# Sigmoid attention and a bilinear feed-forward on one core: sums of the late weights' blocks in buffers of their own, their w_out part stored in 2 KB rows, eight warm-up matmuls, first v on ScalarE's queue

## The chip, the core and the metric

One NeuronCore of a Trainium2 chip runs the kernel as one program. TensorE (PE in the rows, PEld for its weight loads) multiplies into PSUM; VectorE (DVE), ScalarE (ACT) and GpSimd (POOL) do the elementwise work; SyncE (SP) only issues transfers. ScalarE and GpSimd issue transfers too, each in the order of its own queue, and all transfers are moved by the core's 16 DMA engines. Every engine takes its instructions strictly in program order, so an instruction that waits holds up all that stand behind it on its engine. The metric is the device time of one execution in microseconds (us), lower is better.

## The reference

Shapes: q, k, v are 8 x 12 x 448 x 64 (batch, heads, sequence, head size), x has 3584 tokens of 768, w1 and w2 are 768 x 1024, w3 is 1024 x 1024 and w_out 1024 x 768. The weights are given in float64 (their reference arithmetic runs on them), everything else in float32.

```python
scores = scale * np.matmul(q, k.transpose(0, 1, 3, 2)) - np.log(S)
attn = 1.0 / (1.0 + np.exp(-scores))
x = np.matmul(attn, v).astype(np.float32)   # heads side by side: 3584 x 768
a = x @ w1
b = x @ w2
h = a * b @ w3
return (h @ w_out).astype(np.float32)
```

## The kernel before, in words

The program has four stages, which TensorE goes through one after the other.

**Attention** (0 to 257 us in the profile). 48 pairs of heads; for each, scores (L174, L190 for the short last chunk), a sigmoid on ScalarE (L182), and the product with v (L201, L208). The result x goes to DRAM (x_dram). Ahead of the first scores TensorE runs 13 matmuls on a tile of zeros (L318), so that its clock is up when real work begins. The loads of the first four pairs are all issued by SyncE, q and k of a pair and then its v, save k of pair 0, which ScalarE issues. Beside the attention, w1 and w2 are decoded from their float64 words (`piece_load`, `piece_magnitude`, `piece_decode`), split into a high and a low part (each product is made as three float32r matmuls) and summed for the next stage.

**Units** (258.7 to 703.1 us). a = x w1 and b = x w2, and their product g, with Winograd's form of Strassen's scheme: seven block products instead of eight. There are 16 groups (4 token blocks x 4 pairs of column blocks of the result). A group is seven steps, `names` = a11, a12, s3, s2, s1, a22, s4; a step is `unit_step` for two column blocks, each 9 matmuls (L428) into one PSUM bank. VectorE takes the results out of PSUM (`add`, L435): u and v of s2, r of a12 and s1, v of a22, u of s4. ScalarE copies a11's result (L443, tile u). GpSimd multiplies the finished halves (L458 after a22, L463 after s4) and issues the store of g (L465). The step s4 accumulates into the very banks of s1 (`kept`), so its first matmul has to wait until VectorE has read s1's result out of that bank (r of s1).

Beside the units, the late weights w_out and w3 are prepared by a generator, `decode_late`, from which the loop over the groups takes a step at a time (`take(decodes, 1)` at three places of most groups). Each block of 128 x 512 numbers is loaded by SyncE (raw, two buffers), ScalarE makes the magnitude (L84, into a tile f, five buffers), VectorE decodes it in six instructions (L91 to L107). From four decoded blocks b11, b12, b21, b22 of a column block, four sums are made **in place**: t3 = b22 - b12 is written over b12, t2 = b11 + t3 over b11, t1 = b22 - t2 over b22, n4 = b21 - t2 over b21 (L477 for differences, L435 for the sum). The blocks b11, b22 and b21 themselves are needed too, so they are put on a list (`put`, `settled`) and stored to DRAM by GpSimd (`store_settled`, L492) one step of the loop later; a sum over such a block has to wait until the store has read it. The first 12 blocks are w_out's (into wo_dram, whose layout makes each store 512 rows of 512 bytes), the next 16 w3's (into w3_dram, 128 rows of 2 KB each).

**Composition** (703.1 to 761.5 us). The product w3 w_out in seven products (L762), each with operands that `load_factors` loads from wo_dram (L568, L569) and w3_dram (L573), three products ahead, and splits on ScalarE, VectorE and GpSimd.

**Output** (761.5 us to the end). g times the composed weight, again seven products (L821).

What sets the order: in attention the program text sets it for every engine. In the units it sets it for TensorE and SyncE alone, and a list scheduler of the framework orders VectorE, ScalarE and GpSimd from its own estimates of the times; so the place at which a decode or a sum stands in VectorE's queue is the scheduler's choice, and the change moves it. A tile of a pool with n buffers waits for the last readers of the tile n allocations before it.

The lines that the change touches: L70 (layout of wo_dram), L144 to L157 (the table load of the sigmoid, and `load_v`), L268 to L270 (when piece 0 is decoded), L311 to L318 (first loads, warm-up), L442 (buffers of u), L501 to L552 (the sums), L568 and L569 (the factors' loads).

Of the kernel before, what the change touches and what calls it, by code (L numbers as in the profile page):

```python
# [11 lines left out]
F32 = mybir.dt.float32  # L12
F32R = mybir.dt.float32r
U32 = mybir.dt.uint32
AF = mybir.ActivationFunctionType
# [10 lines left out]
def sigmoid_attention_bilinear_ffn(  # L26
# [16 lines left out]
    nc = tc.nc  # L43
    B, H, D, S = qT.shape
    DM, DF = w1.shape[0], w1.shape[1] // 2
    NT = B * S
    P = 128
    CHUNKS = [(c, min(P, S - c)) for c in range(0, S, P)]
    NC = len(CHUNKS)
# [3 lines left out]
    NF = DF // P  # L53
    NM = DM // 2
    NH = NF // 2
# [7 lines left out]
    const = ctx.enter_context(tc.tile_pool(name="const", bufs=1))  # L63
    pw = ctx.enter_context(tc.tile_pool(name="pw", bufs=6))
    dram = ctx.enter_context(tc.tile_pool(name="dram", bufs=1, space=bass.MemoryType.DRAM))
# [1 line left out]
    g_dram = dram.tile([NF, P, NT], F32, name="g_dram")  # L67
    t_dram = dram.tile([NF, 4, P, 2, KH, P], F32, name="t_dram")
    w3_dram = dram.tile([7, NF // 2, P, NF // 2, P], F32, name="w3_dram")
    wo_dram = dram.tile([7, P, NF // 2, NM], F32, name="wo_dram")  # L70
    corner_dram = dram.tile([P, NF // 2, NM], F32, name="corner_dram")

    def split(dst_hi, dst_lo, src, hi_engine, lo_engine):
# [8 lines left out]
    def magnitude(raw, pool, bufs):  # L82
        f = pool.tile([P, *raw.shape[1:-1]], F32, name="f", bufs=bufs)
        nc.scalar.activation(f, raw[..., 1].bitcast(F32), AF.Abs, scale=HW_SCALE)  # L84
        return f
# [38 lines left out]
    pa = phase_a.enter_context(tc.tile_pool(name="pa", bufs=2, side="left"))  # L124
    ps = phase_a.enter_context(tc.tile_pool(name="ps", bufs=3, space=PSUM))

    PLAIN = 1
    pairs = [(b, hp) for b in range(B) for hp in range(NPAIR)]

    def load_pair(p, engines=(nc.sync, nc.sync)):  # L130
        b, hp = pairs[p]
        heads = slice(2 * hp, 2 * hp + 2)
        qk = pa.tile([P, 2, S], F32, name="qk", bufs=6)
        for i, (src, engine) in enumerate(zip((qT, kT), engines)):
            engine.dma_start(out=qk[:, i], in_=src[b, heads].rearrange("h d s -> (h d) s"))
        return qk
# [4 lines left out]
    bias = const.tile([P, 1], F32, name="bias")  # L141
    nc.vector.memset(bias, -math.log(S))

    ready = const.tile([P, 1], F32, name="ready")  # L144
    nc.scalar.activation(ready, bias, AF.Sigmoid)

    def load_v(p):
        b, hp = pairs[p]
        vv = pa.tile([P, NC, 2 * D], F32, name="vv", bufs=6)
        cols = slice(hp * 2 * D, (hp + 1) * 2 * D)  # L150
        full = (NC - 1) * P
        nc.sync.dma_start(
            out=vv[:, :NC - 1], in_=v[b, :full, cols].rearrange("(c p) e -> p c e", p=P)
        )
        rows = slice(p % 2 * D, (p % 2 + 1) * D)
        nc.sync.dma_start(out=vv[rows, NC - 1], in_=v[b, full:, cols])
        return vv  # L157

    def split_pair(p, qk):
# [106 lines left out]

    steps = []
    for i in range(2 * NF):  # L268
        at = 2 + 5 * i // 2
        steps += [(max(at - 3, 0), piece_load, (i,)), (at - 1, piece_magnitude, (i,)), (at, piece_decode, (i,))]  # L270
        steps += [(at + 1, piece_split, (i,))]
        if i % 2:
            steps += [(at + 1, piece_sum, (i // 2, 0)), (at + 2, piece_sum, (i // 2, 3))]
            steps += [(at + 2, piece_sum, (i // 2, 2)), (at + 3, piece_sum, (i // 2, 1))]
# [33 lines left out]
    order.enter_context(tc.manual_schedule(engines={ET.PE, ET.SP, ET.Activation, ET.Pool}))  # L308
    AHEAD = 4
    X_LOADS = 2 * NPAIR + 8  # L310
    qks[1] = load_pair(1)  # L311
    vvs[0] = load_v(0)
    vvs[1] = load_v(1)
    for p in range(2, AHEAD):
        qks[p], vvs[p] = load_pair(p), load_v(p)
    warm = ps.tile([P, 2, 512], F32, name="sp", bufs=3)
    for _ in range(13):
        nc.tensor.matmul(warm[:, 0, :S], zeros[:, :P], zeros, start=True, stop=True)  # L318
    parts = {0: (qks[0],)}
    xs = []  # L320
# [113 lines left out]
    def add(out, a, b):  # L434
        nc.vector.tensor_tensor(out=out, in0=a, in1=b, op=ALU.add)  # L435
# [3 lines left out]
    def unit_step(g, fc, name):  # L439
        acc = x_product(fc, name)  # L440
        if name == "a11":
            us[fc] = pu.tile([P, S], F32, name="u", bufs=3)  # L442
            nc.scalar.copy(out=us[fc], in_=acc)  # L443
        elif name == "a12":
            rs[fc] = pu.tile([P, 2, S], F32, name="r", bufs=3)
            add(rs[fc][:, 0], acc, us[fc])
        elif name == "s3":
            p7s[fc] = acc
        elif name == "s2":
            add(us[fc], acc, us[fc])  # L450
            vs[fc] = pu.tile([P, S], F32, name="v")
            add(vs[fc], p7s.pop(fc), us[fc])
        elif name == "s1":
            add(rs[fc][:, 1], acc, vs[fc])
        elif name == "a22":
            add(vs[fc], acc, vs[fc])
            r = rs[fc]
            nc.gpsimd.tensor_tensor(out=r[:, 1], in0=r[:, 1], in1=vs.pop(fc), op=ALU.mult)  # L458
        else:
            u = us.pop(fc)  # L460
            add(u, acc, u)
            r = rs.pop(fc)
            nc.gpsimd.tensor_tensor(out=r[:, 0], in0=r[:, 0], in1=u, op=ALU.mult)  # L463
            at = 2 * g * S
            nc.gpsimd.dma_start(  # L465
                out=g_dram[fc, :, at:at + 2 * S].rearrange("p (t s) -> p t s", t=2), in_=r
            )
# [8 lines left out]
    def subtract(out, a, b):  # L476
        nc.vector.tensor_tensor(out=out, in0=a, in1=b, op=ALU.subtract)  # L477
# [16 lines left out]
    def decode_late():  # L494
        todo = list(late_sources())
        nxt = [load_words(todo.pop(0), pu, 2) for _ in range(2)]
        yield

        def one():
            raw = nxt.pop(0)  # L500
            f = decode(raw, magnitude(raw, pu, 5))  # L501
            if todo:
                nxt.append(load_words(todo.pop(0), pu, 2))
            return f

        for cb in range(NM // P):
            def put(name, f):
                settled.append((wo_dram[right[name], :, :, cb * P:(cb + 1) * P], f))

            b12 = one()  # L510
            yield
            b11 = one()
            put("b11", b11)
            yield
            b22 = one()
            put("b22", b22)
            subtract(b12, b22, b12)
            put("t3", b12)
            yield
            add(b11, b12, b11)  # L520
            put("t2", b11)
            subtract(b22, b22, b11)
            put("t1", b22)
            b21 = one()
            put("b21", b21)
            yield
            subtract(b21, b21, b11)
            put("n4", b21)
            yield
        for c in range(NH):  # L530
            def put(name, f):
                settled.append((w3_dram[left[name], c], f))

            a21 = one()
            yield
            a11 = one()
            put("a11", a11)
            subtract(a21, a11, a21)
            put("s3", a21)
            yield  # L540
            a22 = one()
            put("a22", a22)
            yield
            subtract(a22, a22, a21)
            put("s2", a22)
            add(a11, a22, a11)
            put("s1", a11)
            a12 = one()
            put("a12", a12)
            yield  # L550
            subtract(a12, a12, a22)
            put("s4", a12)  # L552
            yield

    arenas = (("x1", "x2", "a11"), ("a12", "s3", "s2"), ("s1", "a22", "s4"))
# [3 lines left out]
    def load_factors(i):  # L559
        t0, t1, t2 = (  # L560
            arena_pools.get(tag, px2).tile([P, 6 * S], F32R, name="ar", tag=tag, bufs=1)
            for tag in arenas[i % len(arenas)]
        )
        J = NH - 1
        wide, one = J * NM, NH * P
        out_hi, out_lo = ([t[:, k * w:(k + 1) * w] for t, w in ((t0, wide), (t1, NM))] for k in range(2))
        at = 2 * NM
        nc.sync.dma_start(out=out_lo[0].bitcast(F32), in_=wo_dram[i, :, :J].rearrange("p j m -> p (j m)"))  # L568
        nc.sync.dma_start(out=out_lo[1].bitcast(F32), in_=wo_dram[i, :, J])  # L569
        hi3 = [t1[:, at:at + one], t2[:, :one], t2[:, 2 * one:3 * one], t2[:, 4 * one:5 * one]]  # L570
        lo3 = [t1[:, at + one:at + 2 * one], t2[:, one:2 * one], t2[:, 3 * one:4 * one], t1[:, at + 2 * one:at + 3 * one]]
        for c, lo in enumerate(lo3):
            nc.sync.dma_start(out=lo.bitcast(F32), in_=w3_dram[i, c].rearrange("p j m -> p (j m)"))  # L573
        for hi, lo in zip(out_hi, out_lo):
            split(hi, lo, lo.bitcast(F32), nc.scalar.copy, nc.vector)
        for c, (hi, lo) in enumerate(zip(hi3, lo3)):
            split(hi, lo, lo.bitcast(F32), nc.scalar.copy, nc.gpsimd if c > 1 else nc.vector)

        def moving(k, j):
            t = (out_hi, out_lo)[k]  # L580
            return t[0][:, j * NM:(j + 1) * NM] if j < J else t[1]

        def standing(k, c, j):
            return (hi3, lo3)[k][c][:, j * P:(j + 1) * P]

        loaded[i] = (moving, standing)
# [330 lines left out]
```

## Time and profile before

| what | before |
|---|---|
| median of 3 runs | 968.41 us (966.88 to 973.74) |
| the profiled execution | 971.64 us, its span 969.8 us |
| TensorE busy | 928.5 us (96%) |
| VectorE, ScalarE, GpSimd busy | 714.6, 384.3, 156.8 us |
| mean granted clock of TensorE | 0.981 |
| stages: attention, units, composition, output | 0 to 257, 258.7 to 703.1, to 761.5, to 969.8 us |

The span runs from the first to the last instruction; the execution's own time is 1.84 us longer. Busy TensorE time is counted with each matmul's end as modelled, so a slow matmul counts as busy: time lost to a low clock is not in the 4% that TensorE sits idle. The row of the granted clock stands in tenths in the profile, and by stretch in the view by windows.

### The profile page before, as it was taken

How to read it: one execution, taken by the hardware profiler on the slowest of the kernel's cores; microseconds unless marked ns; L12 is line 12 of the kernel's file. 1: busy time of each engine (PE TensorE's matmuls, PEld its weight loads, DVE VectorE, ACT ScalarE, POOL GpSimd, SP SyncE). 2: the span in 40 equal slices, each digit the busy share in tenths (PEclk: the TensorE clock that was granted, in tenths of full speed). 3: DMA queues.
4: the chain of work that ended last, by engine and by line, in shares of the span. 5: the costliest groups of instructions: out<-in, count | busy, mean ns of one | idle time of the engine just before them, and what ended most of it. 6: DMA issues, size and time to landing. Idle time of an engine off the chain costs nothing.

```text
span 969.8 us, 14374 instructions
## 1 busy us (share of the span) xinstructions
PE 928.5 (96%) x5191; PEld 760.4 (78%) x5191; DVE 714.6 (74%) x1084; ACT 384.3 (40%) x544; POOL 156.8 (16%) x165
## 2 busy tenths in 40 slices
PE   9999999999996798967999999999999999999998
PEld 5455455455695798967999999899999998999997
DVE  5889898986583759727697679756569998777762
ACT  6878878877810013100230113000466544233310
POOL 0000000000031332413323232234344000000000
PEclk9999999999998899987999999999999999999999
DMA  9888999995288465882758866677787367565622
GB/s 298 263 294 288 307 326 322 326 320 199 102 281 326 137 229 178 280 303 99 241 177 300 322 233 204 233 244 238 240 271 255 104 208 245 183 235 183 216 89 86
DMA packets 134134, 227.59 MB, mean 235 GB/s; under 512 B 11632, under 2 KB 100080, under 8 KB 134064
## 3 DMA queue, kind: packets, MB, share of 16 engines
q1 hardware_dynamic: 127152, 197.34, 61.0%
q0 software_dynamic: 6768, 29.10, 8.2%
q8 instruction: 42, 0.69, 0.3%
q14 instruction: 28, 0.23, 0.1%
q10 hardware_dynamic: 144, 0.23, 0.1%
HBM read 163.71 MB, written 62.91 MB: 234 GB/s over the span
## 4 chain that ended last, share of the span: by engine, by line
PE 70%; DVE 13%; issue 8%; DMA 5%; POOL 2%; ACT 2%; DVEq 0%; POOLq 0%; ACTq 0%
PE up L428 26%; PE up L821 16%; PE av L208 11%; PE sp L174 10%; PE av L201 2%; PE sp L190 2%; DMA wo_dram<-f 1%; DVE w L75 1%; DMA ar<-wo_dram 1%; DMA w_dram<-f 1%; DVE u L435 1%; PE up L762 1%; DVE r L435 1%; ACT ar L74 1%; DVE gs L75 1%
## 5 line engine op out<-in xcount | busy, mean ns | idle before, releaser
L428 PE MATMUL up<-xs,tw 128*128 128x448 f32 x864 | 175.7, 362 | 0.2 <-DVE u L435 0.2
L428 PEld LDWEIGHTS up<-xs,tw 128*128 128x128 f32 x864 | 161.9, 187 | 11.4 <-DVE u L435 0.6
L182 ACT ACTIVATE ap<-sp,bias 128x896 f32<-128x896 f32 x168 | 156.2, 1008 | 14.5 <-PE sp L174 10.8
L428 PE MATMUL up<-xa,w 128*128 128x448 f32 x576 | 117.9, 362 | 0.7 <-ACT t L214 0.7
L821 PE MATMUL up<-gs,w 128*128 128x448 f32 x576 | 116.6, 362 | 2.0 <-DVE v L653 2.0
L821 PEld LDWEIGHTS up<-gs,w 128*128 128x128 f32 x576 | 107.9, 187 | 9.6 <-ACT gs L74 2.3
L428 PEld LDWEIGHTS up<-xa,w 128*128 128x128 f32 x576 | 107.9, 187 | 8.6 <-ACT t L214 1.5
L208 PE MATMUL av<-ap,vv 128*64 128x448 f32 x576 | 113.5, 543 | 0.0
L84 ACT ACTIVATE f<-raw 128x512 f32<-128x512 f32 (+1 forms) x44 | 33.8, 769 | 193.2 <-DMA raw<-w3T 124.1
L428 PE MATMUL up<-xs,w 128*128 128x448 f32 x288 | 66.9, 389 | 33.3 <-DVE r L435 33.3
L458 POOL TENSOR_TENSOR r<-r,v 128x448 f32<-128x448 f32 x32 | 42.8, 1357 | 341.3 <-DVE v L435 341.2
L428 PEld LDWEIGHTS up<-xs,w 128*128 128x128 f32 x288 | 58.5, 205 | 39.7 <-DVE r L435 35.1
L208 PEld LDWEIGHTS av<-ap,vv 128*64 128x64 f32 x576 | 39.2, 137 | 63.5 <-issue 54.4
L821 PE MATMUL up<-ga,w 128*128 128x448 f32 x432 | 88.2, 363 | 0.0
L821 PEld LDWEIGHTS up<-ga,w 128*128 128x128 f32 x432 | 81.0, 188 | 6.0
L477 DVE TENSOR_TENSOR f<-f 128x512 f32<-128x512 f32 x21 | 14.6, 697 | 79.9 <-DMA wo_dram<-f 48.2
L428 PE MATMUL up<-xa,tw 128*128 128x448 f32 x288 | 60.2, 362 | 0.0
L762 PE MATMUL up<-ar 128*128 128x384 f32 x336 | 58.4, 334 | 0.0
L762 PEld LDWEIGHTS up<-ar 128*128 128x128 f32 x336 | 58.3, 188 | 0.0
L174 PE MATMUL sp<-qh 64*128 64x448 f32 x282 | 57.7, 406 | 0.0
L428 PEld LDWEIGHTS up<-xa,tw 128*128 128x128 f32 x288 | 54.0, 187 | 3.6
L174 PEld LDWEIGHTS sp<-qh 64*128 64x128 f32 x282 | 26.3, 183 | 37.9 <-issue 31.7
(88 smaller groups left out, 1299.6 us busy)
## 6 DMA issues: line engine op xcount, KB each, us to landing
tw<-t_dram SPq DMA_DIRECT2D x128, 384.0 KB, 5.0
graw<-g_dram SPq DMA_DIRECT2D x60, 448.0 KB, 4.4
g_dram<-r POOLq DMA_DIRECT2D x32, 448.0 KB, 3.1
raw<-w SPq DMA_DIRECT2D x16, 768.0 KB, 6.6
t_dram<-th SPq DMA_DIRECT2D x32, 384.0 KB, 4.4
qk<-qT SPq DMA_DIRECT2D x48, 224.0 KB, 4.7
x_dram<-t SPq DMA_DIRECT2D x48, 224.0 KB, 5.0
xr<-x_dram SPq DMA_DIRECT2D x48, 224.0 KB, 6.1
```

The costliest lines, as they stand in the source:

```text
L75: lo_engine.tensor_tensor(out=dst_lo, in0=src, in1=dst_hi, op=ALU.subtract)
L84: nc.scalar.activation(f, raw[..., 1].bitcast(F32), AF.Abs, scale=HW_SCALE)
L174: nc.tensor.matmul(sp[:, j], qks[kt][rows, 1, at:at + n], qks[qt][rows, 0], start=m == 0, stop=m == len(terms) - 1,)
L182: nc.scalar.activation(a, sp, AF.Sigmoid, bias=bias, scale=scale)
L190: nc.tensor.matmul(sp[i * D:(i + 1) * D, j], qk[rows, 1, S - D:], qk[rows, 0], start=True, stop=True)
L201: nc.tensor.matmul(acc[cols, :S], v[rows, NC - 1, cols], a[rows, j], start=True, stop=False)
L208: nc.tensor.matmul(acc[cols, :S], v[:, c, cols], a[:, j], start=False, stop=c == len(aps) - 1)
L428: nc.tensor.matmul(acc[:, :S], ws[w][:, c], xop[name][x][:, c], start=onto is None and (c, m) == (0, 0), stop=(c, m) == (KH - 1, 2), skip_ ...
L435: nc.vector.tensor_tensor(out=out, in0=a, in1=b, op=ALU.add)
L458: nc.gpsimd.tensor_tensor(out=r[:, 1], in0=r[:, 1], in1=vs.pop(fc), op=ALU.mult)
L762: nc.tensor.matmul(acc[:, :NM], standing(x, c, j), moving(y, j), start=not onto and (j, m) == (0, 0), stop=(j, m) == (NH - 1, 2), skip_gro ...
L821: nc.tensor.matmul(acc[:, :TB], w[:, c, ms], g[:, c], start=first and (c, m) == (0, 0), stop=(c, m) == (NH - 1, 2), skip_group_check=not f ...
```

## The change

It does five things.

1. The four sums of a column block (and of w3's four) go to new tiles of the same pool (`combine`), instead of over their inputs. The pool's tiles f become six instead of five, and to make room the tiles u of the units become two instead of three.
2. wo_dram gets the layout of w3_dram: a block is stored as 128 rows of 2 KB. The factors' loads read it back in four transfers whose pieces are 512 bytes (three of 128 x 3 x 128 for the wide part, one for the last row block), where there were two, of rows of 4.5 KB and 1.5 KB.
3. Eight warm-up matmuls instead of 13.
4. v of the pairs 0 and 1 is issued by ScalarE, ahead of the sigmoid's table load; on SyncE q and k of the pairs 1 to 3 follow one another, then v of the pairs 2 and 3.
5. Piece 0 of w1 is decoded one pair later, and a tile of 64 bytes at the start of the attention's pool moves all its tiles by 64 bytes.

```diff
-    wo_dram = dram.tile([7, P, NF // 2, NM], F32, name="wo_dram")
+    wo_dram = dram.tile([7, NM // P, P, NF // 2, P], F32, name="wo_dram")
...
+    pa.tile([P, 16], F32, name="gap", bufs=1)
...
-    def load_v(p):
+    def load_v(p, engine=nc.sync):
...
-        at = 2 + 5 * i // 2
-        steps += [(max(at - 3, 0), piece_load, (i,)), (at - 1, piece_magnitude, (i,)), (at, piece_decode, (i,))]
+        at = max(2 + 5 * i // 2, 3)
+        steps += [(at - 3, piece_load, (i,)), (at - 1, piece_magnitude, (i,)), (at, piece_decode, (i,))]
...
-    qks[1] = load_pair(1)
-    vvs[0] = load_v(0)
-    vvs[1] = load_v(1)
+    for p in range(2):
+        vvs[p] = load_v(p, nc.scalar)
+    ready = const.tile([P, 1], F32, name="ready")
+    nc.scalar.activation(ready, bias, AF.Sigmoid)
+    for p in range(1, AHEAD):
+        qks[p] = load_pair(p)
     for p in range(2, AHEAD):
-        qks[p], vvs[p] = load_pair(p), load_v(p)
+        vvs[p] = load_v(p)
...
-    for _ in range(13):
+    for _ in range(8):
...
-            us[fc] = pu.tile([P, S], F32, name="u", bufs=3)
+            us[fc] = pu.tile([P, S], F32, name="u")
...
-            f = decode(raw, magnitude(raw, pu, 5))
+            f = decode(raw, magnitude(raw, pu, 6))
...
+        def combine(op, name, a, b):
+            f = pu.tile([P, NH, P], F32, name="f", bufs=6)
+            op(f, a, b)
+            put(name, f)
+            return f
...
-                settled.append((wo_dram[right[name], :, :, cb * P:(cb + 1) * P], f))
+                settled.append((wo_dram[right[name], cb], f))
...
-            subtract(b12, b22, b12)
-            put("t3", b12)
-            yield
-            add(b11, b12, b11)
-            put("t2", b11)
-            subtract(b22, b22, b11)
-            put("t1", b22)
+            t3 = combine(subtract, "t3", b22, b12)
+            yield
+            t2 = combine(add, "t2", b11, t3)
+            combine(subtract, "t1", b22, t2)
             b21 = one()
             put("b21", b21)
             yield
-            subtract(b21, b21, b11)
-            put("n4", b21)
+            combine(subtract, "n4", b21, t2)
...
-        nc.sync.dma_start(out=out_lo[0].bitcast(F32), in_=wo_dram[i, :, :J].rearrange("p j m -> p (j m)"))
-        nc.sync.dma_start(out=out_lo[1].bitcast(F32), in_=wo_dram[i, :, J])
+        wide_lo = out_lo[0].bitcast(F32).rearrange("p (j m) -> p j m", j=J)
+        for cb in range(NM // P):
+            cols = slice(cb * P, (cb + 1) * P)
+            nc.sync.dma_start(out=wide_lo[:, :, cols], in_=wo_dram[i, cb, :, :J])
+        nc.sync.dma_start(
+            out=out_lo[1].bitcast(F32).rearrange("p (b m) -> p b m", b=NM // P), in_=wo_dram[i, :, :, J].rearrange("b p m -> p b m")
+        )
```

The sums of w3's four blocks are changed in the same way as those shown.

**VectorE, second group of the units.** The first column block's last two results stand here: b21 is f_3393 before and f_3392 now, n4 is made from it and t2, and f_3545 is b12 of the second column block; r, u and v are the units' own results that TensorE waits for. Before:

```order
L477 TENSOR_TENSOR f_3326<-f_3326,f_3236 128x512
L103 TENSOR_SCALAR raw_3244<-f_3393 128x512
L104 SCALAR_TENSOR_TENSOR raw_3244<-raw_3244 128x512
L435 TENSOR_TENSOR r_3323<-up_3313,u_3297 128x448
L107 TENSOR_TENSOR f_3393<-f_3393,raw_3244 128x512
L91 TENSOR_SCALAR raw_3334<-raw_3334 128x512
L96 TENSOR_SCALAR f_3545<-f_3545 128x512
L99 SCALAR_TENSOR_TENSOR f_3545<-f_3545,raw_3334 128x512
L103 TENSOR_SCALAR raw_3334<-f_3545 128x512
L104 SCALAR_TENSOR_TENSOR raw_3334<-raw_3334 128x512
L477 TENSOR_TENSOR f_3393<-f_3393,f_3236 128x512
L107 TENSOR_TENSOR f_3545<-f_3545,raw_3334 128x512
```

Now, from the first sums of the column block (t3 is f_3332, t2 f_3388, t1 f_3390):

```order
L479 TENSOR_TENSOR f_3332<-f_3322,f_3168 128x512
L437 TENSOR_TENSOR f_3388<-f_3232,f_3332 128x512
L479 TENSOR_TENSOR f_3390<-f_3322,f_3388 128x512
L91 TENSOR_SCALAR raw_3240<-raw_3240 128x512
L96 TENSOR_SCALAR f_3392<-f_3392 128x512
L437 TENSOR_TENSOR r_3307<-up_3297,u_3281 128x448
L99 SCALAR_TENSOR_TENSOR f_3392<-f_3392,raw_3240 128x512
L103 TENSOR_SCALAR raw_3240<-f_3392 128x512
L104 SCALAR_TENSOR_TENSOR raw_3240<-raw_3240 128x512
L437 TENSOR_TENSOR r_3319<-up_3309,u_3293 128x448
L107 TENSOR_TENSOR f_3392<-f_3392,raw_3240 128x512
L479 TENSOR_TENSOR f_3461<-f_3392,f_3388 128x512
```

The three sums t3, t2, t1 follow each other without the decode of b21 between them, n4 follows right after b21's decode instead of after five of the six instructions of the next block, and no sum names the same tile left and right of the arrow any more. Behind both pieces stand u, v, u, v of s2 and then r of s1, in the same order as before.

**GpSimd, the same place.** Its queue from the store of the first group's second g on (f_3236 before is first b11 and then t2, f_3326 first b22 and then t1, f_3393 first b21 and then n4). Before:

```order
L465 DMA g_dram_64<-r_3120 128x896
L492 DMA wo_dram_67<-f_3326 512x1x128
L492 DMA wo_dram_67<-f_3172 512x1x128
L492 DMA wo_dram_67<-f_3236 512x1x128
L492 DMA wo_dram_67<-f_3326 512x1x128
L492 DMA wo_dram_67<-f_3393 512x1x128 x2
L492 DMA wo_dram_67<-f_3607 512x1x128
L458 TENSOR_TENSOR r_3311<-r_3311,v_3371 128x448
```

Now:

```order
L467 DMA g_dram_64<-r_3116 128x896
L494 DMA wo_dram_67<-f_3322 128x512
L494 DMA wo_dram_67<-f_3332 128x512
L494 DMA wo_dram_67<-f_3388 128x512
L494 DMA wo_dram_67<-f_3390 128x512
L494 DMA wo_dram_67<-f_3392 128x512
L494 DMA wo_dram_67<-f_3461 128x512
L494 DMA wo_dram_67<-f_3607 128x512
L460 TENSOR_TENSOR r_3307<-r_3307,v_3368 128x448
```

The seven stores stand in the same order, ahead of the same multiplication; each is now of 128 rows and from a tile of its own.

**ScalarE and SyncE at the start.** ScalarE's first rows, the difference with numbers of lines as each program has them, before and now:

```order
L135 DMA qk<-kT 128x448
L145 ACT_TABLE_LOAD
L145 ACTIVATE ready<-bias 128x1
L182 ACTIVATE ap<-sp,bias 128x896 x8
L214 COPY t<-av 128x448
L84 ACTIVATE f<-raw 128x768
```

```order
L137 DMA qk<-kT 128x448
L151 DMA vv<-vL 128x3x128
L155 DMA vv<-vL 64x128
L151 DMA vv<-vL 128x3x128
L155 DMA vv<-vL 64x128
L313 ACT_TABLE_LOAD
L313 ACTIVATE ready<-bias 128x1
L181 ACTIVATE ap<-sp,bias 128x896 x8
L213 COPY t<-av 128x448 x2
```

Four transfers of v stand ahead of the table load, and the first magnitude (L84) has gone behind the next seven sigmoids.

## Rows read from the trace of the kernel before

**Rows 1.** The page's first line and its first part: busy time, share of the span and instructions of each engine.

```profile
span 969.8 us, 14374 instructions
PE 928.5 (96%) x5191; PEld 760.4 (78%) x5191; DVE 714.6 (74%) x1084; ACT 384.3 (40%) x544; POOL 156.8 (16%) x165
```

**Rows 2.** Waits over the whole span, of TensorE, VectorE and ScalarE: who waited for whom, us in total, times, longest.

```profile
PE up L428 <- DVE r L435: 33.3, 4, 15.1
...
DVE raw L91 <- ACT f L84: 24.0, 11, 5.2
...
ACT u L443 <- POOL r L463: 30.2, 9, 8.8
```

**Rows 3.** Timeline of TensorE in the units: start, length, instructions, and in brackets the idle time before them and what ended it.

```profile
320.84 5.70 PE L428 MATMUL up<-xs,w 128*128 128x448 f32 x18 [15.06 <-DVE r L435]
...
442.04 6.50 PE L428 MATMUL up<-xs,w 128*128 128x448 f32 x18 [13.65 <-DVE r L435]
...
623.55 4.13 PE L428 MATMUL up<-xs,w 128*128 128x448 f32 x18 [2.15 <-DVE r L435]
627.52 7.36 PE L428 MATMUL up<-xa,w 128*128 128x448 f32 x36
634.72 10.96 PE L428 MATMUL up<-xs,tw 128*128 128x448 f32 x54
...
649.12 3.76 PE L428 MATMUL up<-xs,w 128*128 128x448 f32 x18
```

**Rows 4.** The chain that ended last, in order of time: start, length, what. Two of its stretches on TensorE in the units.

```profile
376.24 23.36 PE up L428 x108
...
442.04 128.97 PE up L428 x630
```

**Rows 5.** Timeline of VectorE around the stalls.

```profile
302.55 0.69 DVE L104 SCALAR_TENSOR_TENSOR raw<-raw 128x512 f32<-128x512 uint32 x1
316.24 0.69 DVE L477 TENSOR_TENSOR f<-f 128x512 f32<-128x512 f32 x1 [13.00 <-DMA wo_dram<-f]
...
320.17 0.62 DVE L435 TENSOR_TENSOR r<-up,v 128x448 f32<-128x448 f32 x1
...
359.83 0.80 DVE L477 TENSOR_TENSOR f<-f 128x512 f32<-128x512 f32 x1 [9.89 <-DMA wo_dram<-f]
...
438.04 0.69 DVE L477 TENSOR_TENSOR f<-f 128x512 f32<-128x512 f32 x1 [18.91 <-DMA wo_dram<-f]
```

**Rows 6.** Timeline of GpSimd: three stores of w_out's blocks, and two of w3's that stand together.

```profile
301.21 0.72 POOL L492 DMA_DIRECT2D wo_dram<-f  x1 [2.66 <-DVE f L107]
306.78 0.71 POOL L492 DMA_DIRECT2D wo_dram<-f  x1 [4.86 <-issue]
313.53 0.72 POOL L492 DMA_DIRECT2D wo_dram<-f  x1 [6.04 <-issue]
...
635.69 1.14 POOL L492 DMA_DIRECT2D w_dram<-f  x2 [0.31 <-DVE f L477]
```

**Rows 7.** Groups of instructions by line over the whole span: busy us, mean ns | idle time of the engine before them, and what ended it.

```profile
L91 DVE TENSOR_SCALAR raw<-raw 128x512 uint32<-128x512 uint32 (+1 forms) x44 | 28.4, 646 | 24.8 <-ACT f L84 24.0 <-DMA x_dram<-t 0.8
...
L443 ACT COPY u<-up 128x448 f32<-128x448 f32 x32 | 16.9, 530 | 98.4 <-PE up L428 68.1 <-POOL r L463 30.2
...
L492 POOL DMA_DIRECT2D w_dram<-f x28 | 15.6, 557 | 101.1 <-DVE f L107 62.0 <-DVE f L477 37.2 <-DVE f L435 1.5
L492 POOL DMA_DIRECT2D wo_dram<-f x21 | 15.2, 723 | 79.4 <-issue 45.0 <-DVE f L107 15.9 <-DVE f L477 9.3
...
L477 DVE TENSOR_TENSOR f<-f 128x512 f32<-128x512 f32 x21 | 14.6, 697 | 79.9 <-DMA wo_dram<-f 48.2 <-DMA w_dram<-f 31.6
```

**Rows 8.** Transfers by issuing line: KB each, median us from issue to landing.

```profile
vv<-vL SPq DMA_DIRECT2D x48, 192.0 KB, 4.2
...
w_dram<-f POOLq DMA_DIRECT2D x28, 256.0 KB, 4.5
...
raw<-w_out SPq DMA_DIRECT2D x12, 512.0 KB, 6.0
wo_dram<-f POOLq DMA_DIRECT2D x21, 256.0 KB, 4.3
```

**Rows 9.** Timeline of the first 10 us.

```profile
1.39 5.22 PE L318 MATMUL sp<-zeros 128*128 128x448 f32 x13 [1.39 <-DVE bias L142]
...
6.54 2.92 PE L174 MATMUL sp<-qk 64*128 64x448 f32 x12
...
8.01 7.37 ACT L182 ACTIVATE ap<-sp,bias 128x896 f32<-128x896 f32 x8 [5.33 <-PE sp L174]
```

**Rows 10.** View by windows, one stretch at the start and one around the first of the four stalls: stretch, then for PE, PEld, DVE, ACT and POOL the busy us and instructions, and last the granted clock of TensorE, the DMA share and GB/s.

```profile
3.00:4.00 1.00, 1.00 (x4) 0.87 (x4) 0.00 (x0) 0.00 (x0) 0.00 (x0) 1.00 1.06 402
...
310.00:322.00 12.00, 1.16 (x3) 1.07 (x4) 5.62 (x11) 0.00 (x0) 1.43 (x2) 0.50 0.70 256
```

**Rows 11.** Timeline of the composition: its matmuls (seven products in a row), and for the factors of the sixth product the first load's issue, ScalarE's cast of what it brought and GpSimd's last splits.

```profile
703.12 58.41 PE L762 MATMUL up<-ar 128*128 128x384 f32 x336
...
727.79 0.32 SPq L568 DMA_DIRECT2D ar<-wo_dram  x1
...
733.82 2.09 ACT L74 CAST ar<-ar 128x1152 fp32r<-128x1152 f32 x3
...
737.49 3.27 POOL L75 TENSOR_TENSOR ar<-ar 128x512 fp32r<-128x512 f32 x2 [5.08 <-ACT ar L74]
```

More of the change, by code (lines that the diff above doesn't have):

```diff
@@ L142, in sigmoid_attention_bilinear_ffn @@
     nc.vector.memset(bias, -math.log(S))
-    ready = const.tile([P, 1], F32, name="ready")
-    nc.scalar.activation(ready, bias, AF.Sigmoid)
-    def load_v(p):
+    def load_v(p, engine=nc.sync):
         b, hp = pairs[p]
@@ L151, in load_v @@
         full = (NC - 1) * P
-        nc.sync.dma_start(
+        engine.dma_start(
             out=vv[:, :NC - 1], in_=v[b, :full, cols].rearrange("(c p) e -> p c e", p=P)
@@ L155, in load_v @@
         rows = slice(p % 2 * D, (p % 2 + 1) * D)
-        nc.sync.dma_start(out=vv[rows, NC - 1], in_=v[b, full:, cols])
+        engine.dma_start(out=vv[rows, NC - 1], in_=v[b, full:, cols])
         return vv
@@ L537, in decode_late @@
             put("a11", a11)
-            subtract(a21, a11, a21)
-            put("s3", a21)
+            s3 = combine(subtract, "s3", a11, a21)
             yield
@@ L543, in decode_late @@
             yield
[L544 to L547, printed above, removed]
+            s2 = combine(subtract, "s2", a22, s3)
+            combine(add, "s1", a11, s2)
             a12 = one()
@@ L550, in decode_late @@
             yield
-            subtract(a12, a12, a22)
-            put("s4", a12)
+            combine(subtract, "s4", a12, s2)
             yield
```

## The prediction

> **What bounds the kernel now.** I read the page's engine shares first: TensorE is busy 928.5 of 969.8 us [rows 1], so a gain must come from the other 41 us or from busy time that is slow. The view of waits puts most of it at one place: TensorE waits 33.3 us in four events for VectorE's r (L435) at L428, the longest 15.1 [rows 2]. The timeline of TensorE places three of them (15.06, 13.65, 2.15 us), each ahead of the 18 matmuls of step s4 [rows 3]; the fourth is the rest, 33.3 − 30.86 = 2.4, ahead of the stretch that starts at 376.24 [rows 4].
>
> VectorE's timeline says why r is late. Before TensorE goes on at 320.84, 376.24 and 442.04, by 4.6, 16.4 and 4.0 us, stands a sum at L477 (316.24, 359.83, 438.04) that had waited 13.00, 9.89 and 18.91 us, always for a transfer into wo_dram [rows 5]. That sum overwrites its own input, which a store must first have read; u, v and r stand behind it on the same engine. After the 13.00, the sum runs at 316.24, r at 320.17, and TensorE goes on at 320.84 [rows 3, 5].
>
> GpSimd's timeline says why the store is late. Of the three w_out stores 301.21, 306.78 and 313.53, the last two waited 4.86 and 6.04 us for nothing but their own issue; two w3 stores go out together in 1.14 us [rows 6]. Over the span that is 45.0 us of "issue" ahead of the 21 w_out stores and none ahead of the 28 others [rows 7]. Both kinds carry 256 KB and land equally long after issue, 4.3 and 4.5 us [rows 8]. So issuing 512 rows holds GpSimd, not the transfer.
>
> A stall also costs afterwards. An undisturbed step of 18 matmuls takes 3.76 us [rows 3], and 36 matmuls start 7.20 apart (627.52 to 634.72), 0.200 each [rows 3]. After the stalls: 5.70 for 18 (+1.94) and 4.13 (+0.37) [rows 3], 23.36 for 108 (21.6, +1.76) and 128.97 for 630 (126.0, +2.97) [rows 4]. The granted clock around the first is 0.50, the 1.2 GHz level, after TensorE had stood idle [rows 10]. Together 7.0 us. The stalls' whole price is 33.3 + 7.0 = 40.3 us.
>
> **The change part by part.**
>
> *Sums in new tiles.* L477 no longer waits for a store to read its operand, so its 48.2 and 31.6 us of idle time [rows 7] have no cause left of this kind. In its place a new tile waits for the readers of the tile six allocations back. A column block now allocates eight tiles (four decoded, four sums) in five takes. A group holds three takes and seven steps of 18 matmuls, 126 × 0.200 = 25.2 us, so five takes are 42 us. Six allocations back is thus about three quarters of a column block, some 30 us; the store was asked to read in one take, some 8 us, and missed by up to 18.91. Even a GpSimd that still took 6 us for each of seven stores would use 42 us, just the length of a column block.
>
> *2 KB rows.* The stores issue like w3's, 0.55 us [rows 7], and GpSimd's 45.0 us of "issue" go. Either part alone should remove most of the stalls; with both I take away all 33.3 + 7.0. What is late next: r of s1 stands behind a decode of six instructions of about 0.4 to 0.7 us, which starts when ScalarE's magnitude is there; L91 has waited for that 24.0 us in 11 events, at most 5.2 [rows 2]. Step s4 can bear about 5.4 us between the end of s1's first bank and its own start (s1's second bank, 9 × 0.200, and a22's 3.6), so most such waits are hidden. Bounds: nothing (the 630 matmuls from 442.04, five groups with decodes in them, ran without a gap [rows 4]), or one wait like the smallest, 2.15 + 0.37 [rows 3], in each of seven column blocks, 17.6. I take one, 2.5 us, as the trace shows one in w3's part, where stores are already wide.
>
> A rule speaks against this account of the slow issue. Rows first: between 302.55 and 316.24 VectorE runs nothing at all [rows 5], and inside that gap GpSimd's two waits of 4.86 and 6.04 fall [rows 6]. The Trainium skill, SBUF — State Buffer, section "SBUF: two separate sides", says that GpSimd cannot write the descriptors of its transfers while VectorE runs certain copies that use both port pairs. By that rule the waits would stay, whatever the rows' width, and the time would be that of rival B below; the trace disagrees, since VectorE stood still while the store waited.
>
> *Two buffers of u instead of three.* a11's copy on ScalarE already waits 30.2 us in nine events for GpSimd's product, at most 8.8 [rows 2], and little of that reaches TensorE, whose idle time without the 33.3 for r and the 1.4 at the start is 6.6 us in all [rows 1, 2, 9]. With two buffers the tile is that of the same column half of the group before, whose product comes right after its s4. Its bank is needed again only some steps later, so the 8.8 is hidden today; I cost 0, and the bound is rival C.
>
> *Composition.* The seven products take 58.41 us, 8.34 each [rows 11]. The sixth must start at 703.12 + 5 × 8.34 = 744.8; its factors are issued at 727.79, cast from 733.82 and split by 740.76, so 4.0 us are free [rows 11]. The loads now come as four of 512-byte pieces and two more issues of 0.32. v's loads in pieces of that width bring 192 KB in 4.2 us [rows 8], against the 6.0 from issue to cast here; so no dearer, 0. If the transfer takes twice as long (+6.0), each of five later products starts 2.0 late: +10.
>
> *Start.* 13 warm-ups take 5.22 us, 0.40 each [rows 9], five fewer are 2.0. TensorE starts the scores at 6.54 right behind them; ScalarE starts at 8.01 and then runs eight sigmoids without a gap [rows 9]. q and k of pair 0 are issued first; at v's 4.2 us from issue [rows 8] they are there by about 5. If the matmuls come up to speed at the same instant as now, 2.0 us of scores run at 0.40 and not at 2.92 / 12 = 0.243 each [rows 9]: five matmuls, 5 × 0.243 = 1.2 us of work. Bounds 0 (data late) and 2.0; I take −1.2.
>
> *v on ScalarE's queue.* From 3 to 4 us the DMA engines are already full (share 1.06, 402 GB/s [rows 10]). v of two pairs, 2 × (192 + 32) KB, is 1.1 us of that, now beside k of pair 1 rather than behind it; that is why I don't take 2.0 above. The Trainium skill, DMA: Bandwidth & Descriptors, section "Issuing engines are not separate DMA queues", says that transfers from several issuing engines interleave on the same 16 engines and only issue time is saved. By it the gain would be about 2.0 − 1.1 = 0.9, and 1.2 without it; the full share agrees with it.
>
> *Piece 0 later, 64 bytes.* Both lie under the attention, and TensorE's idle time outside the four events is those 6.6 us in the whole span: 0. If decoding a pair later were exposed, w1's sums have the whole attention (257 us) to catch up.
>
> Sum on the profiled span: 969.8 − 33.3 − 7.0 + 2.5 − 1.2 = 930.8, an execution of 932.6 with the 1.84 around it. The profiled execution (971.64) lies 3.2 above the median of the runs, so the saving of 39.0 goes off the median: 968.41 − 39.0 = 929.4. I say 930.
>
> **Rivals.**
>
> A. *The decode's own waits take the stalls' place.* For it: L91's 24.0 us [rows 2], and n4 now stands straight behind b21's decode. Against it: s4's slack of 5.4 us covers the longest, 5.2. If in each of seven column blocks a stall like that at 623.55 remains, 17.6 instead of 2.5: 945.
>
> B. *GpSimd's waits aren't the rows' width.* Then stores still go at 6 us each, seven to a column block, 42 of its 42 us: six tiles are not enough, the wait moves from the sum to the next magnitude, and half the stalls stay: 968.4 − 20.2 − 1.2 = 947. Against it: w3's stores, same size, same engine load, at 0.55. If all of it moves, nothing is gained: 967 to 968, the case of no change.
>
> C. *Slower: u with two buffers.* GpSimd's product of s4 stands behind the block's stores in its queue, and these wait for VectorE's sums. If one such store holds the product by more than about 10 us after a11's end, TensorE stands at that bank. The longest wait today is 8.8 [rows 2] with three buffers. The time is lost in each of some 13 groups with decodes: to be slower than before it must lose over 39 / 13 = 3.0 us in each; at 3.5, 45.5 us: 930 + 45.5 = 975. The w_out stores were the slow ones and get faster, which speaks against it.
>
> **How the numbers follow.** Forecast 0.74 (924 to 940), A 0.14 (945), B with half left 0.06 (947), no gain 0.03 (968), C 0.03 (975). The low end is all of 40.3 and 2.0 off the median, 926.1, less the 1.5 by which the fastest run shown is below it: 924. The high end is the composition's +10, 940, plus the same kind of spread: 942, which takes in part of A; beyond it lie at most 2 in 10. About 1% (9.7 us) is what a measurement of this kernel can tell from no change. Faster by more: the forecast, A and B, 0.94; within it 0.03; slower C, 0.03.
>
> **What would show it.** TensorE's list of waits loses r as its first row; at most one wait of 2 to 3 us remains. The sums' line no longer waits for a transfer; GpSimd's w_out stores read 0.55 us with no "issue". The units end at about 703 − 38 = 665, the steps of 18 stay at 3.76, the mean granted clock rises from 0.981. The composition still takes 58.4. The scores start near 4.6 and the first sigmoid near 6 to 7. I am wrong if L91 or a11's copy appears as what TensorE waits behind, if "issue" stays ahead of the stores (B), or if the composition shows gaps before its later products.

## The result and the profile after

The changed kernel takes 930.94 us (median of four runs, 929.08 to 931.25) against 967.82 for the kernel before beside it (966.88 to 973.74): 0.960 of its time, 95% interval 0.956 to 0.964. The forecast was 930.0, range 924 to 942, faster.

The first page of the profile, span and TensorE's share; they answer to [rows 1]:

```profile
span 929.3 us, 14431 instructions
PE 920.7 (99%) x5186; PEld 754.8 (81%) x5186; DVE 713.5 (77%) x1084; ACT 384.8 (41%) x544; POOL 152.7 (16%) x165
```

All waits of TensorE over the span (who waited for whom, us in total, times, longest):

```profile
PE up L826 <- DVE v L658: 2.2, 1, 2.2
PE sp L320 <- DVE bias L144: 1.4, 1, 1.4
PE up L430 <- ACT t L213: 0.7, 1, 0.7
PE up L826 <- DVE u L658: 0.3, 1, 0.3
PE up L430 <- DVE r L437: 0.2, 1, 0.2
```

The first row of [rows 2], 33.3 us for r, is now the last, 0.2. What had made r late is gone too, as the groups by line show (busy us, mean ns | idle time before, and what ended it). L494 is GpSimd's store, L479 VectorE's difference; they answer to [rows 7]:

```profile
L494 POOL DMA_DIRECT2D w_dram<-f x28 | 15.4, 551 | 72.0 <-DVE f L107 67.4 <-DVE f L479 1.8 <-DVE f L437 1.5
L494 POOL DMA_DIRECT2D wo_dram<-f x21 | 11.8, 563 | 38.5 <-DVE f L107 36.3 <-issue 1.4 <-DVE f L437 0.6
...
L479 DVE TENSOR_TENSOR f<-f 128x512 f32<-128x512 f32 x21 | 14.5, 689 | 0.5
```

The w_out stores wait 1.4 us for their issue in place of 45.0, and the sums wait 0.5 us in place of 79.9. The view by windows shows the units before and after (busy us and instructions of PE, PEld, DVE, ACT, POOL, then the granted clock of TensorE, DMA share, GB/s): the granted clock rises from 0.96 to 1.00.

```profile
258.70:703.12 444.42, 410.94 (x2017) 382.54 (x2018) 308.47 (x435) 75.97 (x100) 133.67 (x145) 0.96 0.70 237
```

```profile
257.50:661.67 404.17, 404.01 (x2017) 378.31 (x2018) 310.40 (x435) 77.08 (x100) 129.12 (x144) 1.00 0.76 260
```

Where the time went is told by TensorE's timeline after: the first matmuls of the units, the only step s4 that still waits, and the first matmuls of the composition and of the output.

```profile
257.50 7.48 PE L430 MATMUL up<-xa,w 128*128 128x448 f32 x36 [0.67 <-ACT t L213]
...
304.74 4.13 PE L430 MATMUL up<-xs,w 128*128 128x448 f32 x18 [0.15 <-DVE r L437]
...
661.51 58.41 PE L767 MATMUL up<-ar 128*128 128x384 f32 x336
719.75 21.86 PE L826 MATMUL up<-ga,w 128*128 128x448 f32 x108
```

In the table and below, a stage lasts from its own first matmul to that of the next stage. The last matmul of the units ends 0.16 us after the first of the composition has started, which is where the window above is cut.

| stage of the profiled execution | before | after | change | forecast |
|---|---|---|---|---|
| attention, to the units' first matmul | 258.70 | 257.50 | −1.20 | −1.2 |
| units | 444.42 | 404.01 | −40.41 | −33.3 − 7.0 + 2.5 = −37.8 |
| composition | 58.24 | 58.24 | 0 | 0 |
| output, to the end of the span | 208.44 | 209.55 | +1.11 | 0 |
| span | 969.8 | 929.3 | −40.5 | −39.0 |

The medians differ by 36.9 us and not 40.5, because the profiled execution of before (971.64) lies 3.8 above the median that the result was measured against (967.82), and that of after (931.1) only 0.2 above its own.

### The profile page after: what moved, and what is told of

Read it like the earlier page. It is cut to its first block, busy times and chain, and to the rows that moved or that the text cites. A ratio compares the mean times of both kernels' runs of the same rounds, so it can differ in the third digit from the quotient of the medians.

```text
span 929.3 us, 14431 instructions
## 1 busy us (share of the span) xinstructions
PE 920.7 (99%) x5186; PEld 754.8 (81%) x5186; DVE 713.5 (77%) x1084; ACT 384.8 (41%) x544; POOL 152.7 (16%) x165
## 4 chain that ended last, share of the span: by engine, by line
PE 86%; DVE 8%; ACT 2%; DMA 2%; issue 1%; SPq 0%; ACTq 0%; DVEq 0%
PE up L430 41%; PE up L826 17%; PE av L207 12%; PE sp L173 11%; PE av L200 2%; PE sp L189 2%; DVE w L75 1%; PE up L767 1%; DVE graw L658 1%; DVE gs L75 1%; DMA raw<-w_out 1%; DVE ga L75 1%; DVE wr L658 1%; ACT ar L74 1%; DMA ar<-w_dram 1%
## 5 line engine op out<-in xcount | busy, mean ns | idle before, releaser
L84 ACT ACTIVATE f<-raw 128x512 f32<-128x512 f32 (+1 forms) x44 | 33.9, 771 | 184.0 <-DMA raw<-w3T 121.6
L437 DVE TENSOR_TENSOR u<-up,u 128x448 f32<-128x448 f32 x64 | 39.2, 618 | 31.0 <-PE up L430 31.0
L430 PE MATMUL up<-xs,w 128*128 128x448 f32 x288 | 60.6, 363 | 0.2 <-DVE r L437 0.2
L91 DVE TENSOR_SCALAR raw<-raw 128x512 uint32<-128x512 uint32 (+1 forms) x44 | 28.5, 647 | 38.2 <-ACT f L84 37.9
L430 PEld LDWEIGHTS up<-xs,w 128*128 128x128 f32 x288 | 53.9, 188 | 4.4 <-DVE r L437 0.9
```

The lines of the kernel that those rows point to most:

```text
L91: nc.vector.tensor_scalar(out=high, in0=high, scalar1=0x80000000, scalar2=0x80000000, op0=ALU.bitwise_and, op1=ALU.bitwise_xor,)
L430: nc.tensor.matmul(acc[:, :S], ws[w][:, c], xop[name][x][:, c], start=onto is None and (c, m) == (0, 0), stop=(c, m) == (KH - 1, 2), skip_ ...
```

## The experiments

Stage times are those of each run's own profile; the kernel before takes 444.4 us in the units, the changed kernel 404.0.

**Each half alone.** The 2 KB rows without the new tiles (the factors' loads follow the layout, as in the change):

```diff
-    wo_dram = dram.tile([7, P, NF // 2, NM], F32, name="wo_dram")
+    wo_dram = dram.tile([7, NM // P, P, NF // 2, P], F32, name="wo_dram")
...
-                settled.append((wo_dram[right[name], :, :, cb * P:(cb + 1) * P], f))
+                settled.append((wo_dram[right[name], cb], f))
```

> The kernel before with the 2 KB rows of wo_dram alone; sums stay in place. My theory (the issue of 512 rows makes the store late, either part alone is enough): the w_out stores issue in 0.55 us with no issue wait, the sums still wait for a store's read but for at most about 6 us, as w3's do today; of TensorE's 33.3 us for r no more than two waits of 2 to 3 us stay, time 931 to 938. Rival (being in place is what costs, whatever the rows): the sums' waits stay above 9 us and the stalls at 20 us or more, time above 950.

Measured: 941.9 us, 0.973 of before (0.968 to 0.977); units 413.0. The stores go out without an issue wait, yet more is left than I expected: waits of TensorE, then those of VectorE's sums.

```profile
PE up L428 <- DVE r L435: 7.5, 4, 3.3
```

```profile
DVE f L477 <- DMA w_dram<-f: 31.5, 8, 6.3
...
DVE f L477 <- DMA wo_dram<-f: 19.3, 5, 6.9
```

A store that is issued at once still takes some 5 us from issue to landing (median 5.2 in this run), and a sum in place waits until the store has read: up to 6.9 us, more than step s4 can always bear. Four stalls (7.5 us) and slow matmuls behind them make up the 8.9 us by which these units are longer than the changed kernel's. The rival (being in place costs all) fell too: the rows alone take off 31.4 us of the 40.4.

The new tiles without the 2 KB rows (the diff's `combine`, six f, two u; layout of before):

> The kernel before with new tiles for the sums (six f, two u) alone; w_out stores stay 512 rows of 512 bytes. My theory: GpSimd still waits some 5 to 6 us of issue ahead of each store of a row (45 us in all), but no sum waits for a store; stalls of TensorE for r at most 5 us, time 931 to 938. Rival (six tiles are too few for stores at 6 us each, the wait moves to the next tile f): ScalarE's magnitude or VectorE's sum waits for a store by up to 10 us, about half of the 40 us stays, time 947 to 952.

Measured: 942.8 us, 0.972 (0.969 to 0.975); units 415.9. No sum waits for a store any more (first row below), but ScalarE's magnitude does (11.7 us), and its copy of a11 waits for GpSimd's product, which stands behind the stores:

```profile
L477 DVE TENSOR_TENSOR f<-f 128x512 f32<-128x512 f32 x21 | 14.5, 689 | 0.5
```

```profile
ACT u L443 <- POOL r L463: 111.8, 27, 23.0
...
ACT f L84 <- DMA wo_dram<-f: 11.7, 2, 6.0
```

TensorE waits once for the copy, 3.85 us, and twice for r, 3.1 us together. Timelines of GpSimd, ScalarE and TensorE around the longest stall:

```profile
310.72 0.71 POOL L492 DMA_DIRECT2D wo_dram<-f  x1 [5.31 <-DVE v L435]
316.51 0.72 POOL L492 DMA_DIRECT2D wo_dram<-f  x1 [5.09 <-issue]
319.50 0.71 POOL L492 DMA_DIRECT2D wo_dram<-f  x1 [2.26 <-issue]
323.97 0.72 POOL L492 DMA_DIRECT2D wo_dram<-f  x1 [3.77 <-issue]
324.64 2.29 POOL L458 TENSOR_TENSOR r<-r,v 128x448 f32<-128x448 f32 x2
326.81 1.20 POOL L463 TENSOR_TENSOR r<-r,u 128x448 f32<-128x448 f32 x1
```

```profile
328.04 0.53 ACT L443 COPY u<-up 128x448 f32<-128x448 f32 x1 [22.96 <-POOL r L463]
```

```profile
328.62 6.47 PE L428 MATMUL up<-xs,tw 128*128 128x448 f32 x18 [3.85 <-ACT u L443]
```

This is the mechanism of rival C, in a kernel whose stores are still slow: GpSimd's products (L458, then L463) stand behind the stores, the second u is not free, ScalarE stands idle for 22.96 us ahead of a11's copy, TensorE stalls 3.85. The first of these waits are laid to VectorE's v, but 310.72 to 316.51 is the pace of before [rows 6], and the view names the last event that it sees; I read them as the same issue wait; that is not shown.

**The start alone** (eight warm-ups, v on ScalarE's queue, nothing else):

> The kernel before with the start alone: eight warm-up matmuls, v of pairs 0 and 1 issued by ScalarE, table load behind them. My theory: the units start 1.2 us earlier, 257.5 in place of 258.7, and the four stalls stay as before, time 966 to 969. Rival: the 1.2 us comes from the later piece 0 or from the moved tiles, then the units start at 258.7 here.

Measured: 967.2 us in one run, span 965.5; the stalls stay (31.8 us in four), and the units start at 259.09, not earlier than before and not at the expected 257.5. So in this run the start by itself brought nothing to the units. ScalarE's timeline says where the lead was lost:

```profile
18.19 0.90 ACT L84 ACTIVATE f<-raw 128x768 f32<-128x768 f32 x1 [2.73 <-DMA raw<-w]
19.00 0.50 ACT L211 COPY t<-av 128x448 f32<-128x448 f32 x1
19.41 6.39 ACT L179 ACTIVATE ap<-sp,bias 128x896 f32<-128x896 f32 x7
```

```profile
12.48 4.66 PE av L205 x24
17.14 2.02 PE sp L171 x18
19.16 1.36 PE av L198 x8
20.52 1.02 PE sp L187 x8
...
24.02 4.66 PE av L205 x24
```

The second fence is TensorE's chain. The scores start at 4.67, and the first long product with v at 12.48, 1.8 ahead of before (14.30). Then ScalarE's magnitude of piece 0 waits for its load, the sigmoids stand behind it, and the next long product comes 11.54 later where the other pairs take 10.4. Of the lead 0.7 is left. At 189 stands a wait of 0.42 us for k, which the run with new tiles alone shows there too (0.17), though it has the start of before; the long product behind it, at 192.03, is 0.5 later than before (191.55), so the rest of the lead is lost there:

```profile
189.03 0.97 PE L187 MATMUL sp<-qk 64*64 64x448 f32 x4 [0.42 <-DMA qk<-kT]
```

**Piece 0 as early as before**, all else as changed:

```diff
-        at = max(2 + 5 * i // 2, 3)
-        steps += [(at - 3, piece_load, (i,)), (at - 1, piece_magnitude, (i,)), (at, piece_decode, (i,))]
+        at = 2 + 5 * i // 2
+        steps += [(max(at - 3, 0), piece_load, (i,)), (at - 1, piece_magnitude, (i,)), (at, piece_decode, (i,))]
```

> The changed kernel with piece 0 of w1 decoded as early as before. My theory after the run with the start alone (its second pair of heads lost 1.2 us while ScalarE's magnitude of piece 0 stood waiting for its load ahead of the sigmoids): the scores still start at 4.67, but the second long product with v starts about 11.5 us after the first and not 10.4, and the units start at 258.5 to 259 and not 257.5; time 1 us above the changed kernel. Rival, the prediction's (piece 0 costs nothing): units at 257.5.

Measured: units at 258.24, first long products at 13.06 and 24.26, 11.2 apart, a little less than expected of both. In the changed kernel they are 10.4 apart (12.98 and 23.35), so the late start of piece 0 is worth some 0.8 us. The time, 931.1 us, can't tell that from the changed kernel.

**13 warm-ups**, all else as changed (`range(8)` to `range(13)`):

> The changed kernel with 13 warm-up matmuls. My theory: scores at 6.54, units start 1.2 to 1.5 us later, about 258.8, the rest as in the changed kernel; v on ScalarE's queue alone gains nothing. Rival: the warm-ups don't matter since ScalarE's sigmoids set the pace of the first pairs, then the units start at 257.5.

Measured: scores at 6.54, ScalarE's sigmoids at 8.11, units at 258.45, so the rival fell. The time is 935.0 us in one run, 4 us above the changed kernel; 1.0 of them lies ahead of the units and 2.9 behind the first matmul of the composition, where no part of this edit is (the units take 404.0 us).

**v on SyncE in the order of before, and no 64-byte tile**, each alone, all else as changed:

> The changed kernel with v of pairs 0 and 1 issued by SyncE in the order of before, the table load behind k of pair 0. My theory: which queue issues v is worth little, units start within 0.5 us of 257. Rival: ScalarE's queue is what lets k of the next pairs come early; then a wait for k appears in the first 20 us and the units start at 258 or later.

> The changed kernel without the tile of 64 bytes. My theory: it costs and gains nothing, the units start between 256.4 and 257.5 as in the four runs so far that hold all of the start. If the moved tiles speed the attention's loads, they start at 258 or later.

Measured: units at 257.24 with v on SyncE (930.8 us), at 256.92 without the tile (930.2 us), one run each. Neither can be told from the 256.43 to 257.50 of the other runs with the whole start. So, as far as one profile of each kernel shows it, the start's gain is the warm-ups', kept by piece 0; the other two edits do nothing that shows.

**Half the number of rows** (256 rows of 1 KB per store, and loads that follow this layout), all else as changed:

```diff
-    wo_dram = dram.tile([7, NM // P, P, NF // 2, P], F32, name="wo_dram")
+    wo_dram = dram.tile([7, P, 2, NM // P, 2, P], F32, name="wo_dram")
...
-                settled.append((wo_dram[right[name], cb], f))
+                settled.append((wo_dram[right[name], :, :, cb], f.rearrange("p (a j) m -> p a j m", a=2)))
```

> The changed kernel with w_out's stores as 256 rows of 1 KB. If the issue wait grows with the number of rows, from 0 at 128 to 4.9 to 6.0 us at 512, it is some 2 us here for each store that follows another; if there is a limit that only 512 rows pass, it is 0. Either way the new tiles hide it: time within 3 us of the changed kernel, 928 to 934. If the time rises to 940 or more, the stores' pace sets the stalls even with new tiles.

Measured: 931.5 us, as expected; units 403.3. GpSimd's timeline where four stores follow each other:

```profile
318.96 1.41 POOL L494 DMA_DIRECT2D wo_dram<-f  x2 [4.56 <-DVE f L107]
320.81 0.67 POOL L494 DMA_DIRECT2D wo_dram<-f  x1 [0.44 <-DVE f L437]
325.46 0.68 POOL L494 DMA_DIRECT2D wo_dram<-f  x1 [3.98 <-issue]
```

Neither guess on the issue holds: three go out close together and the fourth waits 3.98. With 512 rows the second one waits. It is not a fixed rule: at 393.32 a fourth store in a row comes 1.30 us after the third, put down to VectorE's r.

**The rows as narrow as before, a store cut in four** (128 rows of 512 bytes each), new tiles kept:

```diff
-                settled.append((wo_dram[right[name], cb], f))
+                settled.extend((wo_dram[right[name], :, j, cb * P:(cb + 1) * P], f[:, j]) for j in range(NF // 2))
```

> The changed kernel with the layout of before for wo_dram and each store of a w_out block cut into four of 128 rows of 512 bytes. If GpSimd's issue wait comes of the number of rows that earlier stores have under way, a block's four stores still hold it 5 to 6 us, and the units take 414 to 424 us. If it comes of the form of one store (512 rows in one instruction), the stores go out in 0.55 us each, 2.2 to 3 us a block, the issue wait is near zero, and the units take 404 to 408 us.

Measured: 931.6 us in one run; units 404.85 (256.79 to 661.64), as the second guess has it. The group of stores:

```profile
L494 POOL DMA_DIRECT2D wo_dram<-f x84 | 46.0, 551 | 20.6 <-DVE f L107 7.1 <-DMA wo_dram<-f 6.0 <-issue 5.6
```

Same bytes, same 512-byte rows, same loads as before, four times the stores: 5.6 us of issue wait in all, 6.0 us of waits for earlier stores, and TensorE waits 0.7 us for r in all. From 390.30 on, 15 stores (1920 rows) leave in 8.19 us without a wait, and only behind them come waits of up to 1.16. So it is neither the width of a row nor the number of rows written, but 512 rows in one store, that held GpSimd.

**Other numbers of buffers.** Five f and three u, once with the 2 KB rows and once with 512 rows per store:

> The changed kernel with five tiles f and three tiles u. If the sixth f matters, ScalarE's magnitude waits for stores and TensorE for r, units 407 to 412 us and the time 933 to 938; if wide rows make five tiles enough, units 404 us and the time 929 to 932.

> The changed kernel with w_out's stores of 512 rows, five tiles f and three u. In the run with new tiles alone the units took 415.9 us, and its longest stall (3.85 us) was a11's copy waiting for a u that GpSimd's product behind the stores kept. If the third u takes that away and five f are enough, the units take 407 to 410 us; if the tiles f are what lacks (magnitude waiting for a store), they take 418 us or more.

Measured: 931.2 us and units 404.5 with wide rows, as the changed kernel; so with prompt stores five f and three u do as well as six and two. With 512 rows per store: 945.8 us, 0.975 (0.972 to 0.977), units 422.5, worse than six f and two u (415.9), as expected if the tiles f are what lacks. Its waits of TensorE and ScalarE:

```profile
PE up L430 <- DVE r L437: 14.5, 2, 12.6
```

```profile
ACT f L84 <- DMA wo_dram<-f: 33.9, 3, 13.9
```

The wait has moved from the sum to the next magnitude, as rival B has it, and VectorE's r comes late behind that.

## Why the prediction was right

*The bound and the stalls.* Right. r's 33.3 us and the 7.0 of slow matmuls make 40.3, and the units lost 40.41. At 0.200 per matmul the 16 groups are 403.2, so only 0.8 of the 404.01 is left.

*The residual.* Mis-sized: I charged 2.5 us for one late r (2.15 of stall and 0.37 of slow matmuls); there is one, 0.15 of stall and 0.37 of slow matmuls. Mainly by this the units gave 2.6 more than the sum had. The output took 1.1 of that back, which I had at 0. From the first matmul of the composition to the end the three programs with sums in place take 266.0 to 266.7 us, nine of the ten with new tiles 267.3 to 268.3 and one (13 warm-ups) 270.7: about 1 us goes with the new tiles. The place can be seen, TensorE's waits for VectorE's u and v early in the output: 1.1 to 2.0 us in those three, 2.0 to 3.6 in those ten. Why VectorE is later there was not found. 40.5 against 39.0 is the difference of these two.

*"Either part alone should remove most of the stalls."* True as it stands: alone they take 31.4 and 28.5 of the 40.4 us off the units. What I built on it was too strong: both expectations (931 to 938) were missed by 4 to 5 us. The step that failed is that a prompt store frees its tile at once, and that 42 us of GpSimd fit in a column block of 42. The two waits are two things: the store's wait to be issued, and the sum's wait for the store to read. In these runs both end only where new tiles and stores of at most 256 rows come together.

*Why the issue was slow.* That GpSimd is held by the issue and not by the transfer or VectorE was right; that width of rows is the cure was only half the story, since four narrow stores of 128 rows do as well. One reading was a little off: of the two waits, 10.9 us, that I put inside VectorE's gap, the first began 1.3 us ahead of it (301.93 against 303.24), so 9.6 us lie inside. The Trainium skill, SBUF — State Buffer, section "SBUF: two separate sides", says that GpSimd cannot write its descriptors while VectorE runs certain operations. The run with four stores speaks against that as the cause here too: VectorE is busy 717.5 us in it, against 713.5 in the changed kernel, and 5.6 of the 45.0 us of issue wait are left.

*The start.* −1.2 was forecast and −1.20 measured, and in this profile by the forecast's own term: the scores start 1.87 us earlier (4.67 for 6.54), and their first 12 take 3.60 us where they took 2.92 [rows 9], which leaves 1.19 (row below). That it agrees to a hundredth is luck: seven programs with eight warm-ups and the later piece 0 start the units at 256.43 to 257.50, four with 13 warm-ups at 258.45 to 259.29, so the gain is 1 to 2.9 us. One term was wrong: I costed piece 0 at nothing since it lies under the attention; without it 0.8 to 1.1 us of the gain is lost again. The cover that I named, w1's sums having 257 us, was the wrong question: ScalarE's place in the queue, not the deadline of the sums, is what moved. v on ScalarE's queue is worth nothing that shows (units at 257.24 without it). The Trainium skill, DMA: Bandwidth & Descriptors, section "Issuing engines are not separate DMA queues", says that issuing from several engines saves only the time of issuing. That run agrees, but the 0.9 and 1.2 that I had with and without this rule are too close to tell apart here.

```profile
4.67 3.60 PE L173 MATMUL sp<-qk 64*128 64x448 f32 x12
```

*Two u, the loads in 512-byte pieces, the 64 bytes.* Nothing, as costed. ScalarE's copy of u waits 63.7 us for GpSimd where it waited 30.2 [rows 2], with the same longest of 8.8, and TensorE sees none of it. The 336 matmuls of the composition take 58.41 us in a row with either form of the loads [rows 11].

```profile
ACT u L445 <- POOL r L465: 63.7, 24, 8.8
...
DVE raw L91 <- ACT f L84: 37.9, 19, 5.2
```

*Rivals.* A did not come: L91 waits 37.9 us for ScalarE (second row above) in place of 24.0 [rows 2], longest 5.2 as before, inside s4's slack. B and C are real mechanisms, shown where 512-row stores were kept; once the stores are prompt neither reaches TensorE, though with four stores per block ScalarE's magnitude still waits 22.4 us for them.

## What to carry to other kernels

A wait that is read as "for a store" has two parts, the time until the store is issued and the time until it has read; look at the issuing engine's own queue first, since one store of many rows can hold all that is behind it. Write a result over its own input only where no transfer has still to read that input. When a stage is started earlier, follow the first loads that other engines take in order: the lead lasts only as far as the first of them that has not moved.

## What the runs showed of the hardware

GpSimd's stores of one 256 KB block leave almost without waiting as one of 128 rows of 2 KB (0.56 us each, 1.4 us of issue wait for 21) or as four of 128 rows of 512 bytes (0.55 each, 5.6 us for 84); as 256 rows of 1 KB a fourth in a row waited 3.98 us in one place; as 512 rows of 512 bytes the second and third in a row waited 4.86 and 6.04 us [rows 6]. What in the chip sets this was not found out.

The first 12 scores took 2.53 to 3.71 us behind eight warm-up matmuls, in programs that don't differ in them, at a granted clock that the view by windows gives as 1.00 from 2 to 10 us. So the start differs by about 1 us between executions, and gains of that size at the start need several profiles.
